# Chunked attention and a bilinear feed-forward: the attention's matmuls on 64x32 tiles of TensorE

## The chip, the core and the metric

The kernel runs on one core of a Trainium2 chip. The metric is the device time of one execution in microseconds (us), here the median over runs. TensorE (PE) does the matmuls, ScalarE (ACT), VectorE (DVE) and GpSimd (POOL) the rest, SyncE (SP) issues most of the transfers. Every matmul is two instructions, a load of the stationary operand (PEld in the profile) and the matmul itself, which streams the columns of the moving operand.

## What is computed

Attention inside chunks of 64 positions, for 8 batches, 8 heads, 576 positions and head width 64; then, with the heads side by side as 4608 tokens of width 512, a bilinear feed-forward of inner width 1536.

```python
q_c, k_c, v_c = (t.reshape(8, 8, 9, 64, 64) for t in (q, k, v))
scores = (1 / 8) * q_c @ k_c.transpose(0, 1, 2, 4, 3)
attn = np.exp(scores - scores.max(-1, keepdims=True))
attn = attn / (attn.sum(-1, keepdims=True) + 1e-9)
x = (attn @ v_c).reshape(8, 8, 576, 64).transpose(0, 2, 1, 3).reshape(4608, 512)
out = ((x @ w_a) * (x @ w_b)) @ w_out
```

## The kernel before

The tokens are cut into nine blocks of 512, each of two units of 256 tokens (four chunks, eight heads). A unit goes through scores, exponential, sums, values and the multiplication by the inverse of the sums; the result is `xT`, the transposed input of the feed-forward, as four tiles (`kt`) of 128 of the 512 columns. The feed-forward of most blocks is a fast matrix multiplication with seven products instead of eight (`side_group`, line 911; `out_seven`, line 1216); the first block's first part is plain (`ffn`, line 822), the last block's output is `out_last` (line 1054).

*Attention matmuls.* The array is used as four tiles of 64x64: the contraction on 64 rows (`j` or `cl` picks the half), the output on 64 partitions. Scores of a unit (`mm_scores`, lines 673 and 685; in the first block `scores_pair`, line 527) are 32 matmuls of 64 columns, one per chunk and head. Sums (`mm_sums`, line 695; `sums_pair`, line 550) multiply the exponentials by a 64x64 block of ones: four matmuls of 512 columns per unit, so that each head's sum stands on the 64 partitions on which its values will stand. Values (`mm_values`, lines 710 and 723; `values_pair`, line 579) are again 32 matmuls of 64 columns, two heads on 64 partitions each. So a column tile of `xT` is two heads of 64.

*The rest of a unit.* ACT takes the exponential of a scores bank of 512 columns (line 787), the logarithm of the sums (line 745, 512 columns twice) and the exponential of its negative (line 747, 1024 columns), which is the inverse; DVE multiplies the values by it into `xT` (lines 764 and 772). In the first block this is done in four pairs of heads (lines 537, 564, 566), and one of the pairs has its inverse from DVE's reciprocal instead (line 560, `RECIP`).

*Weights.* `load_four` (line 413) loads pieces of `w_a` and `w_b` of 256 rows by 512 columns, rows r and r+128 on one partition, and casts them to bfloat16 (line 326, as all copies and casts).

*The order.* All operations are entered into a planner, but their engines, PSUM banks and order come from a table, `ORDER_OF_ALL`, which `follow` reads: a letter for the engine, the operation's number, and its banks; `f` is a matmul of zeros that fills a gap on TensorE (line 1529). Each engine's queue follows this table, SP's loads (line 355) too. Attention matmuls stand in stretches between products of the feed-forward: from the fourth block on two units are done in one joint stretch or in three steps (`attend_two`), with products of the feed-forward between scores, sums and values.

Of the kernel before, what the change touches and what calls it, by code (L numbers as in the profile page):

```python
# [85 lines left out]
c125 e0 b1 e2 d48 b3 e4 b5 e6 d57 b51 b7 f0 f0 f0 f0 f0 f0 f0 f0 a52:0 a49:1 a58:2 b59 c60 a61:3 b62 f4 f4 f4 f4  # L86
a63:45 b64 d66 d69 b65 c53 e11 c50 e9 d75 e8 a67:6 e126 a54:70 c68 a70:2 c71 b56 a76:3 b55 b77 a105:14 c106 a98:50 b99
d78 b100 b101 d85 f6 a72:67 b73 a79:2 b80 c84 f3 f3 f3 f3 f3 f3 f3 a86:3501 b74 b90 b89 b88 c92 c87 c107 e10 d91 e145
a81:62 f7 a111:71 b112 b82 f3 f3 f3 a93:3057 c94 d132 d151 c95 a152:6 c153 b113 b114 a102:14 b83 a118:32 b97 c103 c104
b96 b119 e128 d138 a139:0 a108:75 b120 a133:6 a115:31 b134 b121 a122:24 e12 c110 c109 d13 a182:5 a164:6 c117 a170:7  # L90
e16 d17 e14 e148 b140 e18 e127 c116 a176:1 b15 c123 c124 a177:3 a183:0 b160 a178 c180 e129 a165:2 a184 c186 b135 a166
a171:4 d19 a179 a136:1 a167 c141 a142:5 b168 c181 c169 b143 b137 a172 e20 e22 b174 e24 a185 a173 a161:6 a220:32 b162
b221 b222 d21 c23 a196:5 b198 a188:1 b190 a232:76 b234 b233 b235 a200:3 c175 c25 c258 e26 c27 e146 c154 a192:4 a155:2
a193:5 a201:1 c264 c260 c262 e28 e147 d157 c187 a158:6 a189:7 c270 e30 b156 b29 c31 a204:2 a216:0 c266 c259 b202 c268
d261 b194 e32 b159 b33 a212:3 c191 e34 e150 b35 a239:46 c265 a213:7 d267 c206 c195 a197:2 a205:5 b214 c263 c272 b241
b240 a283:36 b218 a217:4 e149 e130 b163 c199 c207 e131 c144 e274 c215 d269 e36 e276 e226 f0 a236:02 c237 b285 b284
c238 d297 e40 a287:56 b286 c288 c289 a208:3 a209:7 b210 c295 c296 a299:0 d298 d37 e225 a301:2 b300 c211 a343:3 c344
a345:5 b302 c203 a348 b349 a350 b351 a352:6 a354 c219 c346 a361:7 a357 a353:3 b355 d41 b358 a363:1 d273 e38 b230 d39
c356 a369 a374:4 c359 a371 c362 a379 c370 c372 c375 d256 b364 a365 a381 b380 b366 a385 c360 c347 a383:5 e277 a376:6
a367 b382 c373 c271 c377 a407:3 a388 e42 b43 b386 e275 d280 b281 b389 a405:0 a396 b397 c387 a400 c242 c368 e44 d45 e46  # L100
a384:4 a414:6 a392:2 e224 c401 c248 b47 c250 a394:7 c254 d243 b393 e223 b229 c390 a398 a410 a423:5 b411 b395 a424 c406
c244 c255 c251 c245 d391 d249 a402 c408 c403 c399 a416 b417 b425 a435:0 a436 e282 c437 d247 a412 a438 b413 a426 b427
c418 c409 c257 a439 c440 a320:34 b321 e231 a292:10 b293 a419 b420 a430 d378 c431 a415:2 a441:3 a442 b322 a332:16 b294
b334 c421 c404 a312:40 b314 b313 a432 c252 a443 a444 a547:6 c246 a428 b445 a455 e228 e279 e278 b333 b315 b335 a456
c291 c465 c253 e227 c446 c433 d290 a316:04 a336:12 e304 c429 a458 a459 d422 c317 c318 a453:7 a451:0 b452 d434 a559:4
d475 a548 b454 c337 c338 c447 c448 a534 b535 a529:1 c473 c460 c449 a536 b537 a531:2 e305 e303 c469 c470 e325 b549 c530
a540 c541 b309 c532 a538:3 c542 a571:1 a543 c544 b457 d466 d450 d474 a550 d472 b572 e306 a539:2 e326 b551 e308 d310
c545 e324 e323 d329 a573:5 a554 c555 a552 a594 b574 a556 c557 e307 a589:0 b595 c590 b330 a591:3 c592 a596 b597 c553
a600 b601 a598:2 c602 a603 b604 a560 c561 a599:0 c605 a609:3 b610 a607:7 c608 e328 e327 d339 a611 a613 a617 c612 c618
d546 d471 d476 d533 d558 a615 c614 d319 a624:4 e311 a340:10 b341 a629 d606 d467 a562 c616 c630 e331 a500:51 b342  # L110
a492:20 b501 b494 b502 b493 c625 a635 a631 b632 c636 e484 e514 e478 a626:4 a563 a496:50 b495 e508 e482 a518:12 b520
b519 b521 e480 e477 c627 a650 e503 c468 e510 c628 c593 a638 c497 a565:4 a522:25 a566 b651 a633:1 c619 d620 e485 c498
a646:0 a634:7 e461 b564 e488 c524 c637 a567 a568 e463 b639 c523 c642 c644 c640 a648:5 a654 a652 c585 c643 c655 c645
c587 a705:2 d641 a656 e481 b569 b647 e506 a708 c657 b709 e479 e483 b490 a575 a765:1 a576 c649 a710 d489 e487 e464 c653
b711 e505 e513 c706 a714 a703:7 a712:3 a747:2 c621 c704 b715 d622 d658 c570 c577 e504 e486 d499 a717 e462 a713:7 b718
c719 a724 e664 c716 c725 a578 a745:6 a726 c727 a730 b746 b748 c766 a728 c729 b515 e509 e512 c731 a768 a579 a763:0 c764
b769 e582 a721:5 d659 c580 a770 a772:1 d586 a774 b775 a773:3 c771 e663 e507 c776 a777 a781:7 a785 a783:0 b778 c779
c782 d588 d516 d767 a789 c790 a798:4 d707 d660 a791 c792 c799 c732 a803 b786 b784 c720 c793 a805 e511 d525 b804 a787
c788 a809 b806 b810 d661 e491 a526:61 b528 a800:3 c801 c623 b527 a824 e517 a722 b723 a680:41 b681 a672:26 b674 e667
e685 e665 e584 a733:3 a734 a736 a737 c802 d780 c825 c735 b673 b682 a692:46 b675 a676:72 e686 b693 b694 e666 b695  # L120
a696:13 d669 e583 b690 a812 a807:4 c738 a741 a742 a739:6 c677 c813 c811 a826 a808:7 c678 a820:2 e684 e687 b670 c697
c698 e683 c816 c818 d817 d796 e671 c814 d815 c821 a828 a740 c827 b743 c744 c829 a749 a822:1 a750 b751 e756 d662 d819
c823 a837:3 a842 b843 b689 e691 a830 c831 c838 c832 c759 d760 a844 a839:0 c840 a848 b849 a752 a753 a846:4 c850 c754
e688 e668 d794 d835 a858 b845 a851 b859 b852 a912:5 b913 a847:7 c853 d854 a914:3 b915 a862 c863 e868 a937:0 c938 a942
c833 a860 c834 e896 e870 e867 a864 c865 a944 a939:2 c940 e897 e869 e895 d699 a946:6 b943 a948 a700:40 b949 d841 b702
a877:72 b881 b701 b882 c945 a951 b952 a959 d795 d941 d797 d679 a947:0 c950 a963 c960 c861 c964 c953 a955:7 b956
a904:45 a876:21 b878 a961 a957:6 a965 c966 d967 a972:2 b907 b908 d866 d901 b879 b909 b958 a977 c978 c962 c973 a889:4
a890 a903:50 b880 c905 d762 a926:13 c928 e758 e581 a983 a979 a974:2 c906 c929 d761 d933 a855:5 a856 c857 b980 d990
d991 a986 c975 d976 b874 a981:1 b984 b873 a982:0 a994:3 d993 e894 b900 e898 c985 c987 a883:2 a998 a884 a1002 c995 a886
a887 c999 e757 a1000 a996:7 c988 c1003 a1016 a1013:1 c1001 c997 c1014 d836 d992 d989 d954 a1004 c1005 a1018 c1019  # L130
a1011:6 d934 a1020:1 c1012 b888 b1017 a891 a892 c885 c893 a1022 b1023 e871 e899 e872 c1024 a1025 c1006 c1007 a1021:0
d1009 a1086:6 a916 a917 b910 c911 a1036 c1037 c1026 c1027 b1087 d968 a1120 b918 b1121 a1032 a1115:2 c1116 d935 b932
a919 a920 c921 b1033 a1126 e875 a927:51 b930 e902 a1051:23 b1055 b1127 c1008 c1015 c1010 b931 a1088:4 c1089 e1044
e1043 e755 e1070 e1071 d1048 d1028 a1038 c1039 d1040 e1041 d969 d1075 a1124:5 a1034 c1035 b1056 d936 e1042 a1122 b1123
c1128 a1050:21 a1078:03 b1053 b1082 b1081 d970 e1072 a1117:7 a1137 b1138 d1047 b1052 a1029:1 a1141 d971 c1118 c1142
a1077:37 b1054 c1079 a1104:06 a1129 b1130 b1083 a1133:2 a1125:5 c1131 a1030 a1135:3 b1136 c1107 e1045 b1134 c1106
c1080 e924 a1143 a1139 d1170 c1144 a1157 d1119 e1222 c1031 a1150:6 c1151 a1057:0 e1069 e923 e922 a1155 c1158 b1156
a1159:7 a1058 c1140 a1161 b1162 e1068 e925 b1074 e1249 a1152:5 c1153 a1160:6 a1164 b1165 a1060 a1176 c1059 b1177
a1189:4 d1168 a1172:5 d1169 c1163 a1180 c1166 d1167 a1178 a1191:0 a1182 e1046 d1132 d1171 c1173 a1194 c1179 e1219
a1061 b1062 c1183 c1181 b1195 d1145 a1174:2 a1063:3 a1064 b1175 c1111 c1112 c1190 a1200 a1198:6 d1184 b1201 c1192  # L140
c1202 d1193 a1065 a1066 c1067 c1085 a1196 a1199:7 e1248 c1154 d1187 d1148 a1210 b1197 a1203 b1084 a1090 a1266:4
a1264:0 b1265 c1211 a1214 c1215 a1091 e1049 b1204 a1289:5 c1205 a1294 c1295 a1212 c1290 d1146 d1206 d1147 e1073 e1221
b1110 b1092 b1267 a1216 c1217 c1213 b1226 e1247 e1076 a1093 a1094 c1095 c1253 a1296 b1297 a1229:61 b1234 a1105:57
# [30 lines left out]
def kernel(  # L174
# [12 lines left out]
    FP32 = mybir.dt.float32  # L187
# [1395 lines left out]
```

## Time and profile before

| | |
|---|---|
| median of 3 runs | 292.72 us (292.49 to 293.35) |
| the profiled execution | 292.49 us, span 290.7 us |
| granted TensorE clock | 1.00 |
| instructions | 8704 |
| bytes moved | 55.09 MB, mean 189 GB/s |

The span runs from the first to the last instruction; the rest of an execution's time lies around it. The profile's rows give a source line, an engine and an operation, written tile <- read tiles, shape and count. In a group's row the numbers after the bar are the busy time in us, the mean ns of one, and the idle time of the engine before it with what ended it. In a timeline row the first number is the start in us from the span's beginning, the second the time from the first start to the last end of the merged instructions. Matmuls are pipelined and their recorded lengths overlap, so their price is read from the start of one to the start of the next.

### The profile page before, as it was taken

The numbers are of one execution on the slowest core, as the hardware profiler recorded it, in microseconds if no ns is written. First come the engines' busy times: TensorE is split into PE (matmuls) and PEld (weight loads), VectorE is DVE, ScalarE is ACT, GpSimd is POOL, SyncE is SP. The second block draws the span as 40 slices with busy tenths as digits, with TensorE's granted clock in tenths as the row PEclk, the third lists the DMA queues.
The fourth block names the chain that finished last, engine by engine and source line by source line (L and its number), as shares of the span: only waits on it lengthen the run. The fifth ranks groups of instructions, "written<-read, shape, count | busy, mean of one in ns | idle before, by whom it ended". The sixth has DMA issues, their size and how long they took to land.

```text
span 290.7 us, 8704 instructions
## 1 busy us (share of the span) xinstructions
PE 285.5 (98%) x3549; PEld 233.4 (80%) x3549; DVE 246.2 (85%) x433; ACT 176.2 (61%) x307; POOL 185.9 (64%) x180
## 2 busy tenths in 40 slices
PE   7999999999999999999999999999999999999995
PEld 3455458887887888788888878888888888888884
DVE  2778899998999998998988988779988889688583
ACT  3887977966667654866683496558827642332521
POOL 4641338465498298539899879967743685787530
PEclk9999999999999999999999999999999999999999
DMA  7999999899767899976999997997950120012034
GB/s 252 390 398 402 288 297 317 195 244 236 177 132 176 226 242 208 271 167 153 211 244 191 251 220 211 205 243 166 160 116 2 40 106 2 0 68 79 3 145 145
DMA packets 137176, 55.09 MB, mean 189 GB/s; under 512 B 122160, under 2 KB 128432, under 8 KB 137136
## 3 DMA queue, kind: packets, MB, share of 16 engines
q1 hardware_dynamic: 135904, 53.43, 71.9%
q10 hardware_dynamic: 1232, 1.11, 1.1%
q8 instruction: 27, 0.44, 0.6%
q14 instruction: 13, 0.11, 0.1%
HBM read 37.75 MB, written 9.44 MB: 162 GB/s over the span
## 4 chain that ended last, share of the span: by engine, by line
PE 95%; DMA 3%; DVE 0%; POOL 0%; issue 0%; ACT 0%; ACTq 0%
PE F L911 51%; PE F L1216 25%; PE F L822 7%; DMA f<-in_k_dram 3%; PE F L1054 3%; PE F L685 2%; PE F L723 2%; PE F L695 2%; PE F L1529 1%; PE F L501 1%; PE F L630 0%; PE F L579 0%; PE F L673 0%; PE F L550 0%; PE F L710 0%; POOL qkb L326 0%
## 5 line engine op out<-in xcount | busy, mean ns | idle before, releaser
L326 ACT COPY part<-F 128x512 f32<-128x512 f32 x91 | 52.5, 591 | 52.0 <-PE F L911 36.2
L945 POOL TENSOR_TENSOR AB<-AB,bsb 128x512 bf16<-128x512 bf16 x46 | 52.8, 1155 | 21.0 <-DVE wst L1173 7.2
L949 DVE TENSOR_TENSOR bsb<-F,part 128x512 bf16<-128x512 f32 x72 | 49.1, 684 | 8.0 <-PE F L911 4.8
L1173 POOL TENSOR_TENSOR wst<-AB 128x512 bf16<-128x512 bf16 x30 | 34.3, 1155 | 13.4 <-PE F L1216 9.9
L911 PEld LDWEIGHTS <-WA 128*128 128x128 bf16 x384 | 37.1, 98 | 5.5 <-issue 1.1
L911 PEld LDWEIGHTS <-WB 128*128 128x128 bf16 x384 | 37.6, 98 | 4.6
L326 ACT COPY wst<-F 128x512 f32<-128x512 f32 (+1 forms) x40 | 22.1, 557 | 29.7 <-PE F L1216 17.9
L949 DVE TENSOR_TENSOR AB<-F,part 128x512 bf16<-128x512 f32 x48 | 32.8, 684 | 2.0 <-PE F L911 1.4
L1216 PEld LDWEIGHTS <-wst 128*128 128x128 bf16 x288 | 28.0, 98 | 3.7 <-issue 0.4
L1216 PEld LDWEIGHTS <-AB 128*128 128x128 bf16 x288 | 28.1, 98 | 3.5 <-issue 0.2
L911 PEld LDWEIGHTS <-Tb 128*128 128x128 bf16 x288 | 27.6, 98 | 3.9 <-issue 0.5
L911 PEld LDWEIGHTS <-Ta 128*128 128x128 bf16 x288 | 27.7, 98 | 3.6 <-issue 0.3
L911 PE MATMUL F<-wst,Tb 128*128 128x256 bf16 x192 | 28.9, 273 | 0.0
L911 PE MATMUL F<-wst,Ta 128*128 128x256 bf16 x192 | 28.9, 273 | 0.0
L911 PE MATMUL F<-xT,WA 128*128 128x256 bf16 x192 | 28.9, 273 | 0.0
L911 PE MATMUL F<-wst,WA 128*128 128x256 bf16 x192 | 28.8, 273 | 0.0
L911 PE MATMUL F<-wst,WB 128*128 128x256 bf16 x192 | 28.8, 273 | 0.0
L911 PE MATMUL F<-xT,WB 128*128 128x256 bf16 x192 | 28.3, 273 | 0.0
L326 POOL CAST qkb<-f 128x1024 bf16<-128x1024 f32 (+1 forms) x21 | 17.2, 835 | 15.1 <-DVE Tb L859 6.3
L1216 PE MATMUL F<-WO,AB 128*128 128x256 bf16 x192 | 24.6, 273 | 0.0
L326 DVE COPY part<-F 128x512 f32<-128x512 f32 x29 | 19.8, 686 | 2.7 <-PE F L911 2.3
L772 DVE TENSOR_TENSOR xT<-F,inv 128x512 bf16<-128x512 f32 x28 | 18.0, 684 | 2.6 <-ACT inv L747 2.1
(135 smaller groups left out, 561.2 us busy)
## 6 DMA issues: line engine op xcount, KB each, us to landing
f<-in_q_dram SPq DMA_DIRECT2D x32, 256.0 KB, 4.8
f<-in_v_dram SPq DMA_DIRECT2D x32, 256.0 KB, 4.3
f<-in_k_dram SPq DMA_DIRECT2D x28, 256.0 KB, 4.5
out_dram<-osb SPq DMA_DIRECT2D x28, 256.0 KB, 3.2
wst<-in_moe_w_b_dram SPq DMA_DIRECT2D x6, 512.0 KB, 8.4
wst<-in_moe_w_a_dram SPq DMA_DIRECT2D x6, 512.0 KB, 8.7
wst<-in_moe_w_out_dram SPq DMA_DIRECT2D x6, 512.0 KB, 6.1
out_dram<-osb SPq DMA_DIRECT2D x12, 128.0 KB, 2.4
```

What stands on the lines that cost most here:

```text
L326: return A.copy(out=out, in_=in_) if e == "act" else ENG[e].tensor_copy(out=out, in_=in_)
L685: T.matmul(PS[j][cl * 64:cl * 64 + 64, c:c + 64], chunk_of(u, 1, m, j, 2 * g + cl), chunk_of(u, 0, m, j, 2 * g + cl), start=True, stop=True,)
L695: T.matmul(SU[cl][j * 64:j * 64 + 64, :], ones[cl * 64:cl * 64 + 64, :], E[u % 2][cl * 64:cl * 64 + 64, j, :], start=True, stop=True,)
L723: T.matmul(PA[cl][j * 64:j * 64 + 64, c:c + 64], vb[u % 2][cl * 64:cl * 64 + 64, g * 512 + h * 64:g * 512 + h * 64 + 64], E[u % 2][cl * 64 ...
L772: op("dve", c_dve(512), lambda e, cl=cl: V.tensor_tensor(out=x.rearrange("p m (g c t) -> p c g m t", g=2, c=2)[:, cl], in0=f_of(PA[cl]).re ...
L822: T.matmul(f_of(b)[:, 0:n].rearrange("p (u t) -> p u t", u=len(us)), w[ft][:, kt, :], x[:, us[0]:us[-1] + 1, kt, :], start=(kt == 0), stop ...
L911: T.matmul(f_of(bank)[:, q * 256:q * 256 + 256], lhs(2 * g + q, kt), rhs[:, kt, :], start=(first and q == 0 and kt == 0), stop=(q == 1 and ...
L945: op(("dve", "pool"), TIMES, lambda e: ENG[e].tensor_tensor(out=dst, in0=dst, in1=b, op=MULT), r=bk, w=key, prio=-300, fast=True)
L949: op("dve", c_dve(512), lambda e: V.tensor_tensor(out=dst, in0=two(f_of(bank)), in1=two(pab[s][i]), op=ADD), r=[("ps", id(bank)), ("part", ...
L1054: T.matmul(f_of(bank)[:, 0:256], lhs[:, i, h], rhs[:, i, :], start=(first and i == 0), stop=(i == NP - 1), skip_group_check=True)
L1173: op(*long_op(hs), lambda e, i=i, x=x, y=y, o_=o_: ENG[e].tensor_tensor(out=SS[i][:, s], in0=x[:, s], in1=y[:, s], op=o_), r=fts + [(name, ...
L1216: T.matmul(f_of(bank)[:, at:at + 256], lhs[:, i, tt * 128:tt * 128 + 128], rhs[:, i, :], start=(first and at == 0 and i == 0), stop=(i == ...
```

## The change

Scores, sums and values use tiles of 64 rows by 32 columns, so that eight matmuls can stand in the array beside each other:

- each score matmul becomes two, on 32 columns of the keys each (`WIDE = 32`), 64 per unit;
- each value matmul becomes two, one for the even and one for the odd columns of `v`, with four heads on 32 partitions each, 64 per unit;
- the sums become eight matmuls of 256 columns, four heads on 32 partitions each; logarithm and exponential of the inverse then work on 256 and 512 columns instead of 512 and 1024, and the multiplication reads the same inverse for both parities;
- a column tile of `xT` is now the even or odd columns of four heads, so the rows of `w_a` and `w_b` are loaded interleaved, rows 2r and 2r+1 on one partition;
- in the first block sums and values are done per half (four heads) instead of per pair, and the reciprocal on DVE is gone;
- the table `ORDER_OF_ALL` is new.

```diff
+    WIDE = 32
+    SMODE = "64"
...
-    inv = [buf("inv", [128, 2, 512], FP32), part[:, 0:2]] + [buf(f"inv_{i}", [128, 2, 512], FP32) for i in range(INVERSES - 1)]
+    inv = [buf(f"inv_{i}", [128, 2, 256], FP32) for i in range(2)]
...
-                src[half * 256:half * 256 + 256, i * 512:i * 512 + 512].rearrange("(k r) c -> r k c", r=128),
+                src[half * 256:half * 256 + 256, i * 512:i * 512 + 512].rearrange("(r k) c -> r k c", k=2),
...
+    def v_of(n, cl, g, h, par):
+        return vb[n][cl * 64:cl * 64 + 64, g * 512 + h * 64 + par:g * 512 + h * 64 + 64:2]
...
+    def columns(cl):
+        return [slice(cl * 64 + i * WIDE, cl * 64 + i * WIDE + WIDE) for i in range(64 // WIDE)]
...
     def mm_scores(u, PS):
...
+                for i in range(64 // WIDE):
                     for j in range(2):
                         for cl in range(2):
...
                             T.matmul(
-                                PS[j][cl * 64:cl * 64 + 64, c:c + 64],
-                                tk[j * 64:j * 64 + 64, mm, n * 64:n * 64 + 64],
-                                tq[j * 64:j * 64 + 64, mm, n * 64:n * 64 + 64],
+                                PS[j][columns(cl)[i], c:c + 64],
+                                kk[:, i * WIDE:i * WIDE + WIDE],
+                                qq,
...
     def mm_sums(u, SU):
-        for j in range(2):
-            for cl in range(2):
-                T.matmul(
-                    SU[cl][j * 64:j * 64 + 64, :],
-                    ones[cl * 64:cl * 64 + 64, :],
-                    E[u % 2][cl * 64:cl * 64 + 64, j, :],
+        for m in range(2):
+            for j in range(2):
+                for cl in range(2):
+                    at = 32 * (2 * m + j)
...
+                        out = SU[cl][at:at + 32, 0:256].rearrange("p (s g t) -> p s g t", s=2, g=2)
+                        e = E[u % 2][cl * 64:cl * 64 + 64, j, :].rearrange("p (g s m t) -> p m s g t", g=2, s=2, m=2)[:, m]
+                    T.matmul(out, ones[cl * 64:cl * 64 + 64, 0:32], e, start=True, stop=True)
...
     def mm_values(u, PA):
+        for par in range(2):
+            for n in range(4):
+                for m in range(2):
+                    for j in range(2):
+                        for cl in range(2):
...
                             T.matmul(
-                                PA[cl][j * 64:j * 64 + 64, c:c + 64],
-                                vb[u % 2][cl * 64:cl * 64 + 64, g * 512 + h * 64:g * 512 + h * 64 + 64],
+                                PA[cl][32 * (h % 4):32 * (h % 4) + 32, at:at + 64],
+                                v_of(b, cl, g, h, par),
                                 E[u % 2][cl * 64:cl * 64 + 64, j, c:c + 64],
...
     def part_sums(u, prio):
...
-                op("act", c_act(512), lambda e, cl=cl: A.activation(out=inv[NI(u)][:, cl, :], in_=f_of(SU[cl]), func=AF.Ln),
-            op("act", c_act(1024), lambda e: A.activation(out=inv[NI(u)], in_=inv[NI(u)], func=AF.Exp, scale=-1.0),
+                op("act", C256, lambda e, cl=cl: A.activation(out=inv[NI(u)][:, cl, :], in_=f_of(SU[cl])[:, 0:256], func=AF.Ln),
+            op("act", 0.65, lambda e: A.activation(out=inv[NI(u)], in_=inv[NI(u)], func=AF.Exp, scale=-1.0),
...
     def part_values(u, prio):
...
+                    return (x.rearrange("p k (g c t) -> p c k g t", g=2, c=2)[:, cl],
+                            f_of(PA[cl]),
+                            y.rearrange("p (s t) -> p s t", s=2).unsqueeze(2).to_broadcast([128, 2, 2, 128]))
...
+    for hu in range(2):
+        sums_half(hu)
+        values_half(hu)
```

More of the change, by code (lines that the diff above doesn't have):

```diff
@@ L91 @@
[L91 to L100, printed above, removed]
@@ L540, with rows_of, mm_half_sums @@
     C256 = 0.38
-    def sums_pair(m):
-        hu, mm = divmod(m, 2)
-        s = slice(mm * 256, mm * 256 + 256)
-        SU = share("sums", hu, mm)
-        def pe(e):
+    def rows_of(u, h):
+        return slice(32 * (h % 4), 32 * (h % 4) + 32)
+    def mm_half_sums(hu, SU):
+        for mm in range(2):
             for j in range(2):
@@ L558, in sums_pair @@
-        if m in RECIP:
-            for cl in range(2):
-                op("dve", 2.2, lambda e, cl=cl: V.reciprocal(out=inv[hu][:, cl, s], in_=f_of(SU[cl])[:, s]),
-                   r=[("ps", id(SU[cl]))], w=[("inv", hu, mm, cl)], ps=[SU[cl]], prio=R0 + m + 0.3)
-            return
-        for cl in range(2):
-            op("act", C256, lambda e, cl=cl: A.activation(out=inv[hu][:, cl, s], in_=f_of(SU[cl])[:, s], func=AF.Ln),
-               r=[("ps", id(SU[cl]))], w=[("inv", hu, mm, cl)], ps=[SU[cl]], prio=R0 + m + 0.3)
@@ new lines, in of_head, with sums_half @@
+    def of_head(hu, cl, mm, j):
+        return E[hu][cl * 64:cl * 64 + 64, j, mm * 256:mm * 256 + 256]
+    def sums_half(hu):
+        SU = share("sums", hu, 0)
+        op("pe", 0.107, lambda e: mm_half_sums(hu, [f_of(x) for x in SU]), r=[("E", hu, mm, j) for mm in range(2) for j in range(2)], w=[("ps", id(x)) for x in SU], ps=SU, prio=R0 + 2 * hu + 1.3, mode="64")
+        for cl in range(2):
+            op("act", C256, lambda e, cl=cl: A.activation(out=inv[hu][:, cl], in_=f_of(SU[cl])[:, 0:256], func=AF.Ln),
+               r=[("ps", id(SU[cl]))], w=[("inv", hu, cl)], ps=[SU[cl]], prio=R0 + 2 * hu + 1.3)
+        op("act", 0.65, lambda e: A.activation(out=inv[hu], in_=inv[hu], func=AF.Exp, scale=-1.0),
+           w=[("inv", hu, cl) for cl in range(2)], prio=R0 + 2 * hu + 1.3)
@@ L736, in i_keys @@
     def i_keys(u):
-        return [("inv", NI(u), n, cl) for n in range(2) for cl in range(2)]
+        return [("inv", NI(u), cl) for cl in range(2)]
     def part_sums(u, prio):
@@ L771, in post @@
[L771 to L779 removed]
+            hu = u % 2
@@ L799, in slot @@
         for n, (cost, pe, r, banks, after, _) in enumerate(parts):
-            k = dict(mode="64", r=r, w=[("ps", id(x)) for x in banks], ps=banks, after=after)
+            k = dict(mode=modes[n], r=r, w=[("ps", id(x)) for x in banks], ps=banks, after=after)
             if fixed:
@@ L1181, in spared @@
     def spared():
-        return [P.ops[n] for hu in range(2) for x in range(2) for n in P.readers.get(("inv", 1, hu, x), ())]
+        return []
     def out_seven(K, prio, last=False, fixed=False):
```

346 lines of the change are left out of this document (159 added, 187 removed).

## The prediction

> **What bounds the kernel now.** I read the page's busy times and chain first, then busy time by stretch, then the TensorE timeline around the attention steps.
>
> ```profile
> PE 285.5 (98%) x3549; PEld 233.4 (80%) x3549; DVE 246.2 (85%) x433; ACT 176.2 (61%) x307; POOL 185.9 (64%) x180
> ...
> PE 95%; DMA 3%; DVE 0%; POOL 0%; issue 0%; ACT 0%; ACTq 0%
> ```
>
> ```profile
> 0.00:17.50 17.50, 15.57 (x244) 8.08 (x245) 10.28 (x19) 11.09 (x28) 9.54 (x21) 1.00 0.94 334
> 17.50:42.30 24.80, 24.78 (x261) 11.87 (x254) 21.19 (x40) 20.57 (x34) 7.38 (x8) 1.00 1.05 342
> 42.30:120.00 77.70, 77.70 (x1002) 67.22 (x999) 73.50 (x133) 52.43 (x88) 51.39 (x48) 1.00 0.92 219
> 120.00:240.00 120.00, 120.00 (x1628) 104.04 (x1621) 104.03 (x177) 76.48 (x128) 91.33 (x83) 1.00 0.77 171
> ```
>
> The columns after the stretch are its length and the busy time of PE, PEld, DVE, ACT and POOL, then the granted clock, the DMA engines' share and GB/s. From 17.5 us, where the feed-forward products start, to 240 us TensorE is busy all the time at clock 1.00: it waits for nobody. So what an edit is worth after 17.5 us is what it does to TensorE's own time, and what it takes off ACT or DVE there buys nothing. Before 17.5 us loads and a chain over all engines decide.
>
> Next, how long the attention steps hold TensorE. The first number is the start, so the start of the next line minus it is the step's price.
>
> ```profile
> 61.81 0.82 PE L1216 MATMUL F<-TS,wst 128*128 128x256 bf16 x6
> 62.56 0.74 PE L685 MATMUL F<-qkT 64*64 64x64 bf16 x64
> 63.23 0.61 PE L911 MATMUL F<-wst,Ta 128*128 128x256 bf16 x4
> ...
> 64.55 1.47 PE L1216 MATMUL F<-WO,wst 128*128 128x256 bf16 x12
> 65.95 0.63 PE L695 MATMUL F<-E,ones 64*64 64x512 bf16 x8
> 66.51 0.50 PE L911 MATMUL F<-wst,WA 128*128 128x256 bf16 x3
> ```
>
> ```profile
> 117.57 0.45 PE L685 MATMUL F<-qkT 64*64 64x64 bf16 x32
> 117.95 0.61 PE L911 MATMUL F<-xT,WA 128*128 128x256 bf16 x4
> ...
> 119.58 0.44 PE L685 MATMUL F<-qkT 64*64 64x64 bf16 x32
> 119.85 0.39 PE L695 MATMUL F<-E,ones 64*64 64x512 bf16 x4
> ```
>
> ```profile
> 38.45 0.41 PE L695 MATMUL F<-E,ones 64*64 64x512 bf16 x4
> 38.79 1.04 PE L822 MATMUL F<-xT,WA 128*128 128x512 bf16 x4
> ```
>
> 32 score matmuls cost 0.27 us when sums of the same mode follow (119.58 to 119.85) and 0.38 when full-width work follows (117.57 to 117.95): leaving the mode costs 0.11. 64 of them cost 0.67, so 0.56 without leaving. Sums of one unit cost 0.34, of two units 0.56, so a unit's four matmuls of 512 columns are 0.22. Six wide products and entering the narrow mode take 0.75 (61.81 to 62.56), twelve take 1.40 (64.55 to 65.95): a product is 0.108 and entering 0.10.
>
> The question that decides this change is why 32 matmuls of 64 columns take 0.27 us: because four tiles of the array are each busy with eight matmuls in a row, or because TensorE gets instructions no faster. Weight loads show it, as there is one ahead of each matmul.
>
> ```profile
> 62.56 0.11 PEld L685 LDWEIGHTS <-qkT 64*64 64x64 bf16 x4 [0.21 <-issue]
> ...
> 62.56 0.42 PEld L685 LDWEIGHTS <-qkT 64*64 64x64 bf16 x42 [0.21 <-issue]
> ...
> 62.56 0.58 PEld L685 LDWEIGHTS <-qkT 64*64 64x64 bf16 x62 [0.21 <-issue]
> ```
>
> ```profile
> 123.53 0.28 PEld L723 LDWEIGHTS <-vb 64*64 64x64 bf16 x22
> ```
>
> Each is the timeline of a window cut shorter or longer; a load lasts 0.10 to 0.11 us. The first four loads of the scores at 62.56 start within 0.01 us, so a burst of waiting instructions goes out at about 3 ns a pair (load and matmul). Late in the values at 123.14 the loads come evenly: 22 starts in 0.28 less 0.10 us, 21 steps of 8.5 ns. In the scores at 62.56 the 20 loads after the 42nd take 0.16 us, 8 ns each. So after some 32 pairs a stretch lives on a supply of one pair per 8.4 ns. With four tiles this is hardly seen, since 0.27 us over 32 is 8.4 ns as well: the array's pace and the supply's pace happen to agree.
>
> **The change part by part.**
>
> ```profile
> L685 PE MATMUL F<-qkT 64*64 64x64 bf16 x448 | 5.4, 195 | 0.0
> L695 PE MATMUL F<-E,ones 64*64 64x512 bf16 x64 | 5.5, 389 | 0.0
> L723 PE MATMUL F<-E,vb 64*64 64x64 bf16 x448 | 5.4, 194 | 0.0
> ```
>
> *Scores and values on 64x32 tiles.* 448 is 32 for each of 14 units; the units 2 and 3, on lines 673 and 710, have 32 each too. Each becomes 64 pairs of half the width and the same 64 columns. Eight tiles run at once, so the array's own time stays; the instructions double. In the queue order after the start, before: scores in six stretches of 32 and five of 64, values in two of 32 and seven of 64; after: scores in ten of 64 and three of 128, values in two of 64 and seven of 128. Both orders have 27 changes into the narrow mode, so what entering and leaving cost doesn't change.
>
> Before: 8 stretches at 0.27 and 12 at 0.56 are 8.9 us. After, two bounds. Low: the first 32 pairs are in the queue already and go out at the eight tiles' pace, half of 0.27, and the others at 8.4 ns: 64 cost 0.13 + 0.27 = 0.40, 128 cost 0.13 + 0.81 = 0.94; 12 and 10 of these are 14.2, or +5.3. High: 8.4 ns from the first pair, 0.54 and 1.08, together 17.3, or +8.4. Nothing at all is the bound below, if supply follows the array (first rival).
>
> [...]
>
> *Sums.* Four matmuls of 512 columns become eight of 256 on eight tiles: half of 0.22 is saved, less four more issues of 3 ns, so 0.10 in each of 16 units, -1.6 us. If eight tiles don't run at once it is 0.
>
> *ACT.* The reciprocal's logarithm and exponential work on 256 and 2x256 columns.
>
> ```profile
> L745 ACT ACTIVATE inv<-F 128x512 f32<-128x512 f32 x32 | 17.6, 608 | 3.2 <-PE F L695 3.2
> L747 ACT ACTIVATE inv<-inv 128x1024 f32<-128x1024 f32 x16 | 16.8, 1071 | 0.2
> ...
> L566 ACT ACTIVATE inv<-inv 128x512 f32<-128x512 f32 x1 | 0.6, 630 | 0.0
> ```
>
> The exponential goes from 1071 to 630 ns, each logarithm loses less than half of 608: some 0.9 us a unit, hidden under TensorE, which isn't waiting for it: 0. The distance from scores to sums gets a little shorter in the new order (18 products of 0.108 instead of 20 in one joint slot, 1.9 us), and the two exponentials of the first unit take 1.2 us, so this stays covered. If the cover were gone, two score banks would be late and the sums behind them would hold TensorE.
>
> *DVE.* Multiplies keep their form, with the inverse repeated; a value tile's 684 ns could grow by that, but DVE is busy 104 of 120 us and nobody waits on it: 0, with some 13% of slack ahead of a loss. Two reciprocals go from the start (below). *Weights with interleaved rows:* each partition still takes two runs of one row of 512 columns per load, the same bytes and runs: 0.
>
> *The start.*
>
> ```profile
> 0.73 1.99 SPq L355 DMA_DIRECT2D f<-in_q_dram  x4
> ...
> 8.41 0.42 SPq L355 DMA_DIRECT2D f<-in_k_dram  x1
> 8.88 0.46 SPq L355 DMA_DIRECT2D wst<-in_moe_w_b_dram  x1
> ```
>
> ```profile
> 15.98 1.04 POOL L326 CAST WB<-wst 128x1024 bf16<-128x1024 f32 x1 [1.46 <-DMA wst<-in_moe_w_b_dram]
> ...
> 17.22 1.04 POOL L326 CAST WA<-wst 128x1024 bf16<-128x1024 f32 x1 [0.20 <-DMA wst<-in_moe_w_a_dram]
> ```
>
> ```profile
> 17.58 2.00 PE L822 MATMUL F<-xT,WB 128*128 128x512 bf16 x8
> 19.42 1.03 PE L822 MATMUL F<-xT,WA 128*128 128x512 bf16 x4
> ```
>
> The feed-forward starts behind weight casts, and these wait for their loads. From 0.73 to 8.41 SP issues eleven loads of 256 KB ahead of the first weight load; in the new order it is seven. By the 334 GB/s of the first stretch a load is 0.8 us, so that weight piece can land up to 3.1 us earlier. The next three pieces of the first weights have three, two and three loads less ahead of them; the second gates the products as the first did, so 1.6 us is what all of them allow. DVE also loses its two reciprocals here and the sums become two steps instead of four, so the inputs need not be later; the values' two stretches of 64 pairs cost about as much as those of 16, 16 and 32 before. Bounds: -2.5, between what the first piece and the others allow, and 0, if the values' copies or the last v load, which now comes behind that weight load, hold it; I take -1.5.
>
> *Sum.* TensorE: low 5.3 - 1.6 = +3.7, high 8.4 - 1.6 = +6.8 (8.4 if the sums don't gain). The even pace only began after 32 pairs, which speaks for the low end; I take a third of the way up, +4.7. With -1.5 at the start it is +3.2 on the profiled execution's 292.49 (span 290.7 and 1.8 around it): 295.7. The median of the runs, 292.72, is 0.2 above: 295.9.
>
> **The rivals.**
>
> First, *the array's pace*: with eight tiles the pairs come as fast as the tiles take them, 4.2 ns a pair. Then scores and values cost nothing more: -1.6 and -1.5 from 292.7, 289.6. It decides if the supply can go below 0.54 us for 64 pairs. For it: the burst of four in 0.01 us. Against it: two stretches that settle at the same 8 to 8.5 ns, evenly spaced, which tiles that are waiting for work would do and busy ones not. 0.12.
>
> Second, *a restart at each empty queue*:
>
> ```profile
> 122.90 0.41 PE L695 MATMUL F<-E,ones 64*64 64x512 bf16 x4
> 123.14 0.82 PE L723 MATMUL F<-E,vb 64*64 64x64 bf16 x64
> 123.89 0.61 PE L911 MATMUL F<-wst,Ta 128*128 128x256 bf16 x4
> ```
>
> ```profile
> 123.39 0.30 PEld L723 LDWEIGHTS <-vb 64*64 64x64 bf16 x19
> ```
>
> Here 64 values cost 0.75 instead of 0.67, and the slow pairs lie where 32 pairs (four of sums, 28 of values) are through: 19 starts from 123.39 take 0.20 us where 8.4 ns would make 0.15. If every stretch over 32 pairs pays that 0.08, the 22 of the new order add 1.8: 297.7. Against it: the scores at 62.56 pass their 32nd pair smoothly. 0.15.
>
> Third, *the start pays for it*: the new order starts the feed-forward 3.7 us earlier, 13.9 instead of 17.6, and TensorE's cost is at its low end, +3.7: the time stays at 292.7. For it: the shorter chain on DVE and ACT, and four loads fewer. Against it: that is more than the first weight piece can gain (3.1) and twice what the third can. 0.08.
>
> **How the numbers follow.** The forecast, 0.65: 295.9, its own range 293.9 (+3.7 and -2.5) to 299.5 (+6.8 and 0). Rivals 0.12, 0.15 and 0.08. The predicted time is the forecast's; the range 292.5 to 299.5 takes in the restart and the start that pays, and leaves out the first rival and the ends of the bounds. 0.3% (0.9 us) is what a measurement of this kernel can tell from no change. Faster has the first rival and a little of the third, 0.14; same the rest of the third and the forecast's lower edge, 0.08; slower 0.78.
>
> **What would show it.** Right: score stretches of 64 that cost about 0.51 us to the next full-width product and of 128 some 1.05 (0.38 and 0.67 before), with weight loads evenly 8 to 8.5 ns apart over their later part; sums of one unit at about 0.24; TensorE still busy all through from the first feed-forward products, which start near 16 us. Wrong: 64 pairs at 0.38, which is the array's pace; gaps past the 32nd pair, which is the restart; TensorE waiting for ACT or DVE in the middle, which none of these numbers holds.

## The result, and the profile after

The changed kernel takes 316.57 us (median of 4 runs, 314.92 to 317.69), the kernel before 292.68 us in the same measurement (292.49 to 293.35): a ratio of 1.081, 95% interval 1.076 to 1.086. The profiled execution took 314.92 us, span 313.1 us, 22.4 us more than that of before.

The page of the changed kernel, first the engines' busy time, then the granted clock in 40 slices of the span, a transfer queue (packets, MB, share) and the chain that ended last:

```profile
PE 296.5 (95%) x4763; PEld 242.6 (77%) x4766; DVE 244.5 (78%) x438; ACT 175.8 (56%) x319; POOL 164.9 (53%) x158
...
PEclk9969999999999999997999999999999999999999
...
q8 instruction: 37, 0.61, 0.8%
...
PE 92%; issue 3%; DMA 3%; ACT 0%; POOL 0%; DVE 0%; POOLq 0%
```

TensorE is still what the time hangs on, but it now stands still for 16.6 us of the span instead of 5.2, and "issue", time in which it waited for nothing that the profile shows, is 3% of the chain, where it was 0%. In two slices the clock isn't full.

What TensorE waited for in the changed kernel (us in total, times, longest), and its busy time by stretch, with the columns of the prediction:

```profile
PE F L712 <- issue: 4.9, 3, 2.9
PE F L580 <- issue: 2.5, 1, 2.5
PE F L902 <- issue: 2.0, 1, 2.0
```

```profile
17.50:42.30 24.80, 24.65 (x368) 11.74 (x367) 17.87 (x35) 15.79 (x31) 9.06 (x10) 0.91 0.97 315
42.30:120.00 77.70, 73.72 (x1255) 61.48 (x1256) 65.76 (x116) 51.15 (x91) 42.09 (x38) 1.00 0.79 191
120.00:240.00 120.00, 117.07 (x2034) 101.94 (x2032) 96.75 (x167) 72.63 (x130) 74.84 (x68) 0.99 0.77 181
```

Before, the two stretches from 42.3 to 240 us were full; now 4.0 and 2.9 us are missing in them, and none of it is a wait for DVE, ACT, POOL or a transfer of data. The timeline of TensorE shows a few long holes. Two of them, one inside feed-forward products (line 902) and one inside a stretch of values that has long begun:

```profile
105.36 1.36 PE L712 MATMUL F<-E,vb 64*32 64x64 bf16 x128
106.66 0.50 PE L902 MATMUL F<-xT,Tb 128*128 128x256 bf16 x3
109.16 0.27 PE L902 MATMUL F<-xT,Tb 128*128 128x256 bf16 x1 [2.00 <-issue]
109.27 0.82 PE L1207 MATMUL F<-wst,AB 128*128 128x256 bf16 x6
...
137.79 1.27 PE L712 MATMUL F<-E,vb 64*32 64x64 bf16 x123
142.00 0.24 PE L712 MATMUL F<-E,vb 64*32 64x64 bf16 x5 [2.93 <-issue]
142.18 1.04 PE L902 MATMUL F<-xT,Ta 128*128 128x256 bf16 x4
143.00 1.06 PE L902 MATMUL F<-wst,WA 128*128 128x256 bf16 x4
```

Between the 123rd and the 124th of 128 values nothing starts for 3.1 us. From start to start there are six such gaps: 2.74 us at 13.17, 1.40 at 48.05, 0.91 at 79.50, 2.27 at 106.89, 3.13 at 138.87 and 0.52 at 246.26, 11.0 us together. Behind the longest, four products take 0.82 us (142.18 to 143.00) instead of the 0.44 of full clock; the stretch says why (clock in the third column from the right):

```profile
142.00:144.70 2.70, 2.70 (x17) 1.91 (x17) 0.60 (x1) 0.00 (x0) 0.00 (x0) 0.50 0.03 6
...
17.50:21.40 3.90, 3.90 (x63) 1.11 (x60) 1.90 (x6) 1.11 (x4) 1.04 (x1) 0.50 1.05 403
```

2.7 us at half clock lose 1.35. The gap of 2.27 us left the clock full (the product at 109.16 is followed by the next after 0.11). Half clock lasts 3.42 us here (141.36 to 144.78), and TensorE was busy for 1.12 of the 3.41 us ahead of it. Around the gap of 2.27 us it was busy for 1.48, and the clock stayed full:

```profile
107.23:110.64 3.41, 1.48 (x14) 1.32 (x14) 1.31 (x3) 0.00 (x0) 1.15 (x1) 1.00 0.79 209
137.95:141.36 3.41, 1.12 (x131) 1.00 (x104) 1.29 (x2) 3.36 (x6) 0.00 (x0) 1.00 0.55 126
141.36:144.78 3.42, 2.78 (x18) 1.98 (x18) 0.68 (x2) 0.00 (x0) 0.00 (x0) 0.50 0.02 5
```

The part that was forecast, the price of the stretches, is there too. A stretch of 64 scores, with its loads as three windows that start alike and end at 72.25, 72.3 and 72.6 us:

```profile
72.03 0.68 PE L679 MATMUL F<-qkT 64*32 64x64 bf16 x64
72.64 1.05 PE L1207 MATMUL F<-wst,wst 128*128 128x256 bf16 x8
```

```profile
72.03 0.22 PEld L679 LDWEIGHTS <-qkT 64*32 64x32 bf16 x33 [0.21 <-issue]
72.03 0.36 PEld L679 LDWEIGHTS <-qkT 64*32 64x32 bf16 x38 [0.21 <-issue]
72.03 0.57 PEld L679 LDWEIGHTS <-qkT 64*32 64x32 bf16 x64 [0.21 <-issue]
```

33 loads lie in the first 0.22 us, only five more start by 72.3, and the 26 after these need 0.21 us (the ends 0.36 and 0.57): 8.1 ns each. So 32 pairs go out fast, then there is a pause until about 0.23 us from the start, and then the even supply of the prediction. 64 pairs cost 0.61 us to the next wide product, where 32 cost 0.38.

### The profile page after: what moved, and what is told of

Same layout as the page of the kernel before. It is cut to its first block, busy times and chain, and to the rows that moved or that the text cites. A ratio compares the mean times of both kernels' runs of the same rounds, so it can differ in the third digit from the quotient of the medians.

```text
span 313.1 us, 11126 instructions
## 1 busy us (share of the span) xinstructions
PE 296.5 (95%) x4763; PEld 242.6 (77%) x4766; DVE 244.5 (78%) x438; ACT 175.8 (56%) x319; POOL 164.9 (53%) x158
## 4 chain that ended last, share of the span: by engine, by line
PE 92%; issue 3%; DMA 3%; ACT 0%; POOL 0%; DVE 0%; POOLq 0%
PE F L902 48%; PE F L1207 24%; PE F L813 7%; PE F L679 3%; PE F L712 3%; PE F L1045 3%; DMA f<-in_q_dram 2%; DMA f<-in_k_dram 1%; PE F L697 1%; PE F L1517 1%; PE F L502 1%; PE F L580 0%; PE F L529 0%; PE F L630 0%; POOL qkb L327 0%
## 5 line engine op out<-in xcount | busy, mean ns | idle before, releaser
L936 POOL TENSOR_TENSOR AB<-AB,bsb 128x512 bf16<-128x512 bf16 x39 | 44.9, 1157 | 35.1 <-DVE AB L940 7.7
L1164 POOL TENSOR_TENSOR wst<-AB 128x512 bf16<-128x512 bf16 x27 | 30.9, 1155 | 18.0 <-DVE AB L936 7.8
L327 ACT COPY wst<-F 128x512 f32<-128x512 f32 (+1 forms) x43 | 24.5, 574 | 27.5 <-PE F L1207 16.2
L764 DVE TENSOR_TENSOR xT<-F,inv 128x512 bf16<-128x512 f32 x32 | 21.0, 685 | 6.4 <-PE F L712 5.9
L1207 PE MATMUL F<-WO,AB 128*128 128x256 bf16 x192 | 25.7, 276 | 0.0
L327 POOL CAST qkb<-f 128x512 bf16<-128x512 f32 (+1 forms) x15 | 12.0, 809 | 24.0 <-DMA f<-in_k_dram 9.0
L327 ACT CAST qkb<-f 128x1024 bf16<-128x1024 f32 (+1 forms) x25 | 23.8, 965 | 0.0
```

The source lines that it names most:

```text
L327: return A.copy(out=out, in_=in_) if e == "act" else ENG[e].tensor_copy(out=out, in_=in_)
L764: return V.tensor_tensor(out=out, in0=in0, in1=in1, op=MULT)
L936: op(("dve", "pool"), TIMES, lambda e: ENG[e].tensor_tensor(out=dst, in0=dst, in1=b, op=MULT), r=bk, w=key, prio=-300, fast=True)
L1164: op(*long_op(hs), lambda e, i=i, x=x, y=y, o_=o_: ENG[e].tensor_tensor(out=SS[i][:, s], in0=x[:, s], in1=y[:, s], op=o_), r=fts + [(name, ...
L1207: T.matmul(f_of(bank)[:, at:at + 256], lhs[:, i, tt * 128:tt * 128 + 128], rhs[:, i, :], start=(first and at == 0 and i == 0), stop=(i == ...
```

## The experiments

**The theory and its rivals.** The queue of instruction transfers moved 0.61 MB in 37 packets, 16 KB each. The program's 9534 loads and matmuls over 37 packets are about 256 each. Theory: TensorE's program comes in blocks of 256 instructions; in stretches of narrow pairs a block is used up in little over 1 us, faster than the next one arrives, and TensorE stops. Rivals: the holes belong to the instructions at which they stand (a wait of the values, or the loads of every second column of `v`); they come from the new table; or the shape of the tiles makes them.

**The same program, 128 instructions later.**

```diff
-        "fn": lambda e: T.matmul(F[at], zero[:, 0:128], zero, start=True, stop=True),
...
+        if count["fill"] != 1:
+            return lambda e: T.matmul(F[at], zero[:, 0:128], zero, start=True, stop=True)
...
+            for i in range(65):
+                c = i % 4
+                T.matmul(F[at][32 * c:32 * c + 32, 0:16], zero[0:64, 0:32], zero[0:64, 0:16], start=True, stop=True)
```

> The changed kernel with 65 tiny pairs (load and matmul of zeros, 16 columns) in place of the first matmul of zeros at the start: every later TensorE instruction stands 128 places further back in the program, half a block of the 256 by which instructions are fetched; all work, order and waits stay. Theory (fetch): the six long gaps of TensorE (13.17, 48.05, 79.50, 106.89, 138.87, 246.26) are waits for the next block of instructions, about 4 us after the one before it was entered; so they leave these instructions and come at others, wherever 256 instructions now fall into less than 4 us; with that rule on the old starts their sum goes from 11 to about 7 us, and the time to 309 to 314. Rival (place): the gaps belong to what stands there (values that wait for another engine, strided loads of v): the same instructions wait as long as before, 316.6 within 1.

309.88 us (309.27 to 311.55), ratio 1.058, interval 1.055 to 1.061. TensorE's waits, and its timeline at the values that had the longest gap:

```profile
PE F L712 <- issue: 3.2, 2, 1.7
PE F L630 <- issue: 2.3, 1, 2.3
```

```profile
132.89 0.69 PE L712 MATMUL F<-E,vb 64*32 64x64 bf16 x59
135.27 0.75 PE L712 MATMUL F<-E,vb 64*32 64x64 bf16 x69 [1.68 <-issue]
```

All six gaps have left their instructions. Four others have come: 0.69 at 12.90 (sums), 2.53 at 16.98 (line 630, in the first block), 1.87 at 133.39 and 1.68 at 216.91 (values), 6.8 us together. The 128 values that stopped after 123 pairs now stop after 59: 64 pairs or 128 instructions earlier, as the shift has it. The time fell by more than the 4.2 us of gaps, since no gap in the middle brings half clock any more and the feed-forward starts at 20.16 instead of 21.39. Waits and loads that belong to these instructions are out.

**256 instructions later.** The same edit with `range(129)`.

> The changed kernel with 129 tiny pairs in place of the first matmul of zeros: every later TensorE instruction stands 256 places further back, one whole block, so the blocks are cut at the same instructions as in the changed kernel. Theory (fetch): the gaps come back to where they were, in values of the first block, in the values near 48, 80 and 139 us and in the feed-forward behind the values near 107 us, 9 to 12 us in all, and the time is 315 to 318. Rival (65 tiny pairs helped in another way, by warming the clock or moving the start): more of them help as much, 308 to 311, with gaps where the shift of 128 had them.

317.51 us (315.06 to 318.21), ratio 1.082, interval 1.077 to 1.087: the changed kernel's time again. Its timeline at the same values:

```profile
140.93 1.25 PE L712 MATMUL F<-E,vb 64*32 64x64 bf16 x123
144.45 0.21 PE L712 MATMUL F<-E,vb 64*32 64x64 bf16 x5 [2.27 <-issue]
```

A whole block of extra instructions brings every gap back to its instruction, here after the 123rd of 128 values as in the changed kernel, with two small ones more (0.60 at 43.70 and 0.74 at 76.69); 12.5 us in all, a little over the expected 9 to 12. Half clock follows two gaps in the middle here, of 2.46 us at 108.19 and 2.47 at 141.98.

**Instructions alone, at the start.** In the kernel before:

```diff
+        if count["fill"] != 8:
+            return lambda e: T.matmul(F[at], zero[:, 0:128], zero, start=True, stop=True)
...
+            for i in range(640):
+                j, c = i // 4 % 2, i % 4
+                T.matmul(F[(at, 7)[j]][32 * c:32 * c + 32, 0:64], zero[64 * j:64 * j + 64, 0:32], zero[64 * j:64 * j + 64, 0:64], start=True, stop=True)
```

> The kernel before, with 640 pairs of zeros on 64x32 tiles, 64 columns each, in one stretch at the start in place of the eighth matmul of zeros, so that nothing but instructions can be late. Theory (fetch): 1280 instructions are five blocks; each 256 run in about 1.1 us (128 pairs at 8.4 ns) and then wait for the next block, so a step of 3.5 to 4.5 us per block and four or five gaps of 2.5 to 3.4 us, 14 to 20 us in all. Rival (supply alone): 640 pairs at 8.4 ns, 5.4 us without a gap.

317.97 us (one run). TensorE's timeline, and the stretch as a whole (the last three figures are the clock, the share of the transfer engines and GB/s):

```profile
4.36 1.98 PE L1537 MATMUL F<-zero 64*32 64x64 bf16 x216
11.32 1.28 PE L1537 MATMUL F<-zero 64*32 64x64 bf16 x128 [4.98 <-issue]
17.51 1.27 PE L1537 MATMUL F<-zero 64*32 64x64 bf16 x128 [4.92 <-issue]
...
29.63 0.54 PE L1537 MATMUL F<-zero 64*32 64x64 bf16 x40 [4.65 <-issue]
```

```profile
4.00:30.00 26.00, 6.53 (x641) 5.68 (x640) 0.48 (x1) 0.62 (x1) 4.06 (x7) 0.60 0.94 331
```

This is the plainest view of it: 128 pairs, which are 256 instructions, and then 4.9 us of nothing, over and over, four gaps in all. A block takes 6.2 us (11.32 to 17.51), more than the 3.5 to 4.5 expected, and the 640 pairs 25.8 us (4.36 to 29.63 and 0.54).

**Instructions alone, near the end.** The same stretch some 22 us ahead of the end:

```diff
-a1602 a1616 a1614 c1615 a1532:0 d1472 d1513 c1603 a1550:7 a1551 c1610 c1474 c1612 c1599 a1642:6 a1619:4 a1533 a1544:1
+a1602 a1616 f0 a1614 c1615 a1532:0 d1472 d1513 c1603 a1550:7 a1551 c1610 c1474 c1612 c1599 a1642:6 a1619:4 a1533 a1544:1
...
+        if count["fill"] != 26:
```

> The kernel before, with the same 640 pairs of zeros in one stretch, but some 22 us ahead of the end, where the chip's transfers are nearly done. At the start, beside transfers of 330 to 400 GB/s, each block took 6.2 us. Theory A (the fetch waits behind the kernel's own transfers): here a block takes well under that, 2.5 to 4.5 us, and the 640 pairs cost 12 to 18 us. Theory B (the turnaround is the fetch's own): 6.2 us per block again, 25 us.

312.22 us (one run). Its timeline, the transfers between 265 and 282 us, and the clock:

```profile
265.75 1.85 PE L1537 MATMUL F<-zero 64*32 64x64 bf16 x204
269.98 1.22 PE L1537 MATMUL F<-zero 64*32 64x64 bf16 x128 [2.38 <-issue]
273.44 1.28 PE L1537 MATMUL F<-zero 64*32 64x64 bf16 x128 [2.24 <-issue]
276.89 1.27 PE L1537 MATMUL F<-zero 64*32 64x64 bf16 x128 [2.18 <-issue]
...
280.93 1.04 PE L911 MATMUL F<-wst,Tb 128*128 128x256 bf16 x4
```

```profile
q8 instruction: 5, 0.08, 1.8%
```

```profile
268.00:274.00 6.00, 1.78 (x197) 1.65 (x198) 0.00 (x0) 0.00 (x0) 0.00 (x0) 0.88 0.01 3
274.00:280.00 6.00, 1.99 (x214) 1.72 (x198) 0.00 (x0) 0.00 (x0) 0.00 (x0) 0.50 0.02 5
```

With nothing else on the transfer engines but five packets of 16 KB, a block takes 3.46 us (269.98 to 273.44); beside 331 GB/s at the start it took 6.2. So theory A holds: a block comes later beside the kernel's own transfers. The 640 pairs took 15.2 us (265.75 to 280.93), within the expected 12 to 18. And 128 pairs take 1.22 us at nearly full clock (269.98) and 1.27 at half clock (276.89): the supply of pairs hardly follows the array's clock.

**Scores and values back on 64x64.** `WIDE = 64`, and the values' loops as before, onto 64 partitions.

> The changed kernel with scores and values back on 64x64 tiles, 32 matmuls per unit each; sums, table and weight rows stay changed. The values land at places that the rest does not expect, so the output is not the reference's. Theory (fetch): with 7230 load and matmul instructions instead of 9534 no 256 of them fall into 4 us, so no gap over 0.3 us, and the time is that of before less 1.6 for the sums and 0 to 1.5 for the start: 289 to 291.5. Rival (the new order): if the table's waits or the interleaved weights cost, the time stays over 295. Rival (supply alone): the same 289 to 291.5, but then the gaps of the changed kernel have no cause.

292.18 us (291.98 to 292.70), ratio 0.9965, interval 0.995 to 0.998. No wait of TensorE for "issue" is left, so neither the table nor the interleaved weights make the gaps. The feed-forward begins at 16.77 instead of 17.58. The gain of 1.1 us is smaller than expected: the new table has moved 12 transposes (0.86 us from start to start) and 32 values of the first block (0.40) behind the first feed-forward product, so the earlier start is paid back there.

**Scores alone back on 64x64.**

```diff
-    WIDE = 32
+    WIDE = 64
```

> The changed kernel with its scores back on 64x64 tiles (32 matmuls per unit); values and sums stay on 64x32. Supply: ten score stretches of 64 and three of 128 go from about 0.62 and 1.18 us to 0.38 and 0.67, 3.9 us less. Theory (fetch): the gaps become fewer too, as only stretches of 128 values still come near 256 instructions in 4 us: 1 to 6 us of gaps instead of 11, so 302 to 308. Rival (supply alone, gaps tied to the values where they are): 312.7.

299.61 us (299.20 to 300.22), ratio 1.022, interval 1.020 to 1.024: below the expected range. Its waits for issue:

```profile
PE F L630 <- issue: 1.2, 1, 1.2
PE F L902 <- issue: 0.7, 1, 0.7
```

Two gaps, 1.46 and 0.98 us, are left, and the clock is 1.00 all through. Its 2.4 us of gaps are what was expected; the range left out what goes with the gaps, the half clock and the late start (the feed-forward begins at 17.64 here, at 21.39 in the changed kernel).

**Values alone back on 64x64.** The values' loops as before, scores narrow.

> The changed kernel with its values back on 64x64 tiles, 32 matmuls per unit; scores and sums stay on 64x32. The values land at places that the rest does not expect, so the output is not the reference's. The value stretches go from 128 and 64 pairs to 64 and 32, about 4 us less. Theory (fetch): few gaps are left, 0 to 4 us, 297 to 302, about as the kernel with the scores put back; gaps, where they come, at a block's end and not tied to values. Rival (the step-2 loads of the narrow values hold TensorE): putting back the values takes far more than putting back the scores did, below 295.

301.69 us (300.84 to 301.78), ratio 1.028, interval 1.026 to 1.030. The gaps come in scores and in feed-forward products now, 1.76 us at 15.45, 0.70 at 71.27 and 0.68 at 231.91: the narrow values are not what makes them. Either half of the change, put back, takes 15 to 17 us off, though the supply of each is worth some 4.

**The kernel before, scores and values twice.** In `mm_scores`, `mm_values` and the first block's two functions:

```diff
-                            T.matmul(
...
+                            for _ in range(2):
+                                T.matmul(
```

> The kernel before, with every score and value matmul issued twice into the same place: as many instructions as the changed kernel, but 64x64 tiles, whole rows of v, the old table and the old sums. Theory (supply and fetch): stretches of 64 and 128 pairs at 8.4 ns cost about 0.55 and 1.08 us plus 0.11 to leave, +8.4, and gaps of 0.5 to 3 us come where 256 instructions fall into less than 4 us, 3 to 11 us in all: 304 to 312. Rival (the tiles' shape, the step-2 loads of v or the new table cause the gaps): no gap over 0.3 us, 300 to 302.

308.71 us (307.01 to 311.51), ratio 1.054, interval 1.047 to 1.061. One of four gaps (2.66, 0.82, 0.96 and 0.58 us) in TensorE's timeline:

```profile
184.89 1.16 PE L729 MATMUL F<-E,vb 64*64 64x64 bf16 x110
186.82 0.37 PE L729 MATMUL F<-E,vb 64*64 64x64 bf16 x18 [0.77 <-issue]
```

The gaps come on 64x64 tiles, with whole rows of `v` and the old table too. It is the number of instructions that brings them, not their shape.

**The same instructions, spread out.** Only the table differs from the changed kernel's; one of ten places:

```diff
-b135 b209 d258 a274:13 b276 b275 c210 a200:4 a227:62 c229 c228 d288 b277 a278:03 c280 c279 e36 b37 e267 e217 a196:1
-a354:7 c286 c287 a290:2 a292:6 b291 a336:3 c260 e40 e216 e266 a334:0 b293 a339 c337 c202 b340 a341 b342 b41 c335 e38
+b135 b209 d258 a274:13 b276 b275 c210 a200:4 a227:62 c229 c228 d288 b277 e36 b37 e267 e217 a196:1 a354:7 a290:2 a292:6
+a278:03 c279 c280 c286 c287 b291 a336:3 c260 e40 e216 e266 a334:0 b293 a339 c337 c202 b340 a341 b342 b41 c335 e38
```

> The changed kernel with another order alone: in each of the ten joint stretches of 128 score or value pairs the second unit's 64 go some two microseconds of feed-forward products later. The same 9534 load and matmul instructions; ten more changes of mode at 0.21 us, +2.1. Theory (fetch): 256 instructions now seldom fall into less than 4 us, so 0 to 3 us of gaps are left of 11, and the half clock behind the longest goes too: 306 to 311. Rival (supply alone, whatever stands together): the supply per pair is the same and the added mode changes are paid: 318.7.

323.16 us (321.25 to 323.81), ratio 1.102, interval 1.098 to 1.105: the forecast of the time failed. TensorE's longest waits:

```profile
PE F L902 <- DVE xT L764: 6.4, 7, 1.5
PE F L697 <- ACT E L777: 4.0, 4, 1.7
PE F L580 <- issue: 2.8, 2, 1.4
```

The gaps did go: behind 44 us not one wait for issue of half a microsecond is left. But what was moved back is multiplied later on DVE and later through ACT's exponential, and TensorE waits for those instead. So the spread shows that the gaps can be taken out of the middle by order alone, and not what the time would then be.

**Where the gaps stand.** In nine kernels (the one with scores and values put back has none) there are 38 gaps of more than 0.5 us that come from no wait for data. (Steps of 0.53 to 0.58 us near the start are long matmuls at half clock and aren't counted.) The profile names nothing that ended 36 of them; two of the kernel before with scores and values twice, at 182.00 and 214.36, it puts down to operations of DVE and ACT, but they stand at the same place of the count as the others. The loads and matmuls recorded ahead of each, counted from the start and divided by 256, leave:

```
changed kernel              190 188 184 184 184 184
128 later                   191 191 187 187
256 later                   191 191 191 187 187 187 187 187
scores back                 191 187
values back                 191 187 187
before, twice               191 186 186 186
spread                      191 191 191
640 pairs at the start      191 191 191 191
640 pairs near the end      185 185 185 185
```

All lie between 184 and 191, in nine programs; where gaps stood anywhere, the remainders would be spread over 256. (Some records are missing from a trace, 5 of the changed kernel's 9534, so later counts come out a few short.)

**The packets themselves.** The traces also hold the time of every packet of the instruction queue. Between 139.6 and 140.6 us, within the longest gap of the changed kernel, there is one:

```profile
q8 instruction: 1, 0.02, 5.5%
```

The last packet ahead of the end of each of the changed kernel's six gaps (us):

| the gap begins | packet starts | packet ends | TensorE goes on | after the packet |
|---|---|---|---|---|
| 13.17 | 13.58 | 14.46 | 15.91 | 1.45 |
| 48.05 | 47.14 | 48.10 | 49.45 | 1.34 |
| 79.50 | 77.96 | 78.83 | 80.41 | 1.57 |
| 106.89 | 106.85 | 107.89 | 109.16 | 1.27 |
| 138.87 | 139.66 | 140.54 | 142.00 | 1.46 |
| 246.26 | 244.46 | 245.51 | 246.79 | 1.28 |

All 38 gaps end 1.26 to 1.57 us after a packet has. In the two long stretches a packet takes about as long (0.93 to 0.97 us at the start, 0.89 to 1.27 near the end) and TensorE goes on as soon after it; what differs is when it starts, counted from the first pair of the block ahead: 3.7 to 3.8 us at the start (11.32 to 15.11), 1.0 to 1.1 near the end (269.98 to 271.02). So in these two it is the wait ahead of the packet that the other transfers go with, not a slower packet.

What starts a fetch was not shown. Counted from the first matmul of the block ahead, the changed kernel's packets start between 1.7 us before it (184.40, matmul at 186.08) and 3.8 us after it. An estimate: TensorE begins to take up a block some 32 pairs ahead of its first matmul, as many as go out at once at 72.03, and where wide products of 0.109 us run these are 3.5 us. Counted from that moment, the earliest packet starts after 1.2 us in the changed kernel (255.67, from 254.50) and after 1.3 in the kernel before.

## Why the prediction was wrong

Forecast 295.9 us, with a range from 292.5 to 299.5; measured 316.6.

- *What fails is the step "So after some 32 pairs a stretch lives on a supply of one pair per 8.4 ns".* It took that supply as endless. It ends with each block of 256 instructions: 128 pairs use a block in 1.2 to 1.3 us, and blocks follow each other in 3.5 to 6.2. In the kernel before a block never ran out: its blocks lasted 5.7 us and more, and 14 where all of it is wide products of 0.109 us. It was close once: the block that begins near 174.5 us had its packet 1.6 us earlier. The row was on the page before:

```profile
q8 instruction: 27, 0.44, 0.6%
```

- 7098 loads and matmuls over 27 packets are 263 each: about the size of a block could have been read there, and 128 values in one stretch are exactly one block.
- *The price of scores and values* was right in kind and too low. Twelve stretches of 64, which were of 32, rose from 0.378 to 0.615 us to the next wide product, and ten of 128, which were of 64, from 0.669 to 1.22 on the mean with the gaps taken out (1.15 to 1.44 in the six that have none): 2.8 + 5.5 = +8.3, against the +6.3 taken and bounds of 5.3 and 8.4. The low bound had the shape, but not the pause of some 0.1 us past the 32nd pair. That pause is what the second rival had (0.08 for each of 22 stretches): low bound and rival together make 7.1. Some of the stretches of 128 have further pauses, of 0.07 to 0.18 us.
- *The sums* came as forecast: eight cost 0.235 us where four cost 0.342, sixteen 0.345 for 0.558, 0.107 for each of 16 units, -1.7.
- *ACT, DVE and the weights* cost nothing, as forecast: a value tile's multiplication takes 685 ns (684 before), and none of the changed kernel's waits in the middle is for them.
- *The start*: 0.8 us earlier with scores and values put back (1.5 taken, bounds 0 and 2.5), and even that is no gain, as the work that the table moved behind it costs 1.3. In the changed kernel the gap of 2.74 us at 13.17 and half clock behind it put the feed-forward at 21.39, 3.8 us later than before.
- *The first rival*, the array's pace, is out: 8.1 ns a pair in the trace, and hardly more at half clock.

Of the profiled 22.4 us, 3.8 lie ahead of the first feed-forward product, the gap of 2.74 among them. From there to the last matmul TensorE took 288.3 us instead of 269.6, 18.7 more. Added up from start to start, the other five gaps are 8.2, scores, values and sums 6.9 (the 8.3 and -1.7 above, and 0.3 beside them), the half clock behind the longest gap 1.35, the moved work 1.5 (12 transposes 0.86, 64 values of the first block 0.65), and the first products 0.9, by half clock until 21.9 us and short waits; this is the 18.7 within 0.2.

What stays open: in the changed kernel the block that begins near 215.5 us ran through in 2.8 us without a gap, and the one ahead of the gap at 48.05 in 4.5, so no single number of microseconds decides. The packets' times go with that. Wide products stood ahead of the first of the two, by the estimate above it was taken up from 212.0 on, and the packet for the block after it started at 215.87 and ended at 216.80, 1.5 us before it was needed. For the other the packet started only 3.6 us after the first pair (43.52 to 47.14). Why the wait differs was not taken apart. With the simple rule of 4 us the sum of gaps after the shift was right (7 expected, 6.8 measured), their places not all. Nor was it tried whether a better table could keep the gaps out without new waits. None of the versions with the reference's output beats the kernel before: without any gap, supply and sums alone leave +6.6 us.

## What to carry to other kernels

TensorE's instructions were here a resource with two limits: a pace per pair (8.1 to 8.4 ns), and a block that has to arrive. When an edit multiplies instructions, count the shortest time in which one block's worth (here 256) will be used anywhere, beside the time for which the trace shows such a block to last today (5.7 us and more before the change) and the time in which one is fetched (here 3.5 us in quiet, 6.2 under load), and look for the row of instruction transfers on the page. If "issue" waits appear in the middle of a queue, shift the program by half a block: here all six gaps left their instructions with 128 more ahead of them, and came back with 256.

## What the runs showed of the hardware

- TensorE's program arrived in packets of 16 KB (37 of them, 0.61 MB, for the changed kernel's 9534 loads and matmuls), and a long stretch of pairs stopped after every 128 of them, which are 256 instructions: for 2.2 us per block in quiet and 4.9 beside 331 GB/s of the kernel's own loads (3.46 and 6.2 us a block). TensorE went on 1.3 to 1.6 us after the packet's end in all 38 gaps.
- Load and matmul pairs came every 8.1 to 8.4 ns, hardly slower at half clock (128 in 1.22 us at nearly full clock and in 1.27 at half); the first 32 pairs of the changed kernel's stretch at 72.03 went out faster (33 loads of 0.09 us within 0.22), with a pause until about 0.23 us from its start.
- In the changed kernel the granted clock fell to half at 15.07 us for 6.83 and at 141.36 for 3.42, and the 119.46 us of full clock between are 35 times 3.41. Ahead of the two falls TensorE was idle for 2.25 us of 3.41 (11.66 to 15.07) and for 2.29 (137.95 to 141.36); with 1.93 (107.23 to 110.64) the clock stayed full. The length of a gap alone didn't decide: behind one of 2.47 us (256 later, at 141.98) four products took 0.67 us instead of 0.44, and with one of 2.66 (before, twice, at 18.35) the clock was 1.00 over the whole run.
